# Attention and gated MLP on one core: weights converted in pieces of 1024 words, all orders new

## The chip, the cores and the metric

The kernel runs on one NeuronCore of a Trainium2 chip. Five engines work side by side: TensorE (PE, matrix multiplications), VectorE (DVE), ScalarE (ACT), GpSimd (POOL) and SyncE (SP, which here issues the DMAs). [...] The metric is device time in microseconds; a profiled execution also has a span, from its first instruction to its last.

## The reference

There are 8 batches of 8 heads, 576 tokens, head width 64. For each head:

```
scores = q @ k.T / 8, causal, + min(-(cum_i - cum_j), 0)    # cum: running sum of max(s, 0)
attn   = softmax(scores);  x = attn @ v
```

The heads of a batch are joined to x (576 x 512), and then

```
h    = max(x @ w_in, 0)                                     # 512 -> 1024 features
gate = sigmoid(conv over 3 tokens of h, weights conv_w per feature)
out  = (h * gate) @ w_out                                   # 1024 -> 512
```

q, k, v and s are float32. w_in, conv_w and w_out come as float64, and the kernel turns them into float32 on the chip.

## The kernel before, in words

**Stages.** 64 heads are worked as 32 pairs (`pair`, line 965): the score matmuls for the row maximum (line 1107), the maxima on DVE (lines 1124 and 1144), the scores again with the maximum subtracted (line 1231), the exponential on ACT (line 1248), the sums (line 1334) and the product with v (line 1282), then the division and the split of x into a high and a low part. After every four pairs a batch is complete; `moe_h` (line 1428) multiplies x with w_in (line 1447), applies the convolution (lines 1485 and 1501), the sigmoid (1516) and the product (1522) and splits the result into u (lines 1531 and 1536); `moe_o` multiplies u with w_out (line 1601). Matmuls are done in three products of high and low parts, so weights too are held as a high part in the matmul's rounded format and a low part, the rest: `wi` and `wo`.

**Converting the weights.** `weight_piece` (line 820) makes a chain of tasks for one piece. SP loads the float64 words into a staging buffer (line 845), each word as two 32-bit halves. ACT takes the absolute value of the upper halves (851), DVE or POOL raises it to a floor (855), DVE shifts it (861), puts the sign in (867) and the top bits of the lower half (873). ACT or DVE then writes the high part (909 for w_in, 930 for w_out), POOL or DVE the low part (912 and 933). DVE alone can do lines 861, 867 and 873. w_in is converted in 8 pieces, one for each tile of 128 features, 512 words wide in each partition. w_out is converted in 12: feature tiles 4 to 7 as pieces of 512 words, tiles 0 to 3 in two halves of 256 words. Pieces of 512 words use three buffers `w`, pieces of 256 words (and the small conv_w) three buffers `ht`. A buffer is free again when its piece's last step is done.

**Who needs them.** The matmuls of `moe_h` for two feature tiles need the pieces of both. The first write of u in batch 0 waits for all pieces (`first`, line 1528), because u lies in the memory that the staging buffers give back.

**The order.** Every instruction belongs to a task with a due time: a formula, plus a shift from the table `DUE`, found by a search. `Sched.play` imitates the engines: at each moment an engine takes the ready task that is due first and whose buffers are free, and where a task may run on several engines, the one that comes to it first. The order that results is written out for every engine before the kernel is built; the engines keep to it. If PE has nothing ready, an idle matmul (line 1667) is put in. SP's loads wait for the first bias rows (`dq0`), except a few early ones, among them the w_in pieces named in `FIRST`, here 5 and 6.

Of the kernel before, what the change touches and what calls it, by code (L numbers as in the profile page):

```python
# [29 lines left out]
FIRST = (5, 6)  # L30
# [65 lines left out]
    "pads":  # L96
        "0 141.6 1 -96.93 2 30.09",
    "ind":
# [400 lines left out]
def kernel(  # L499
# [404 lines left out]
    for f in range(NF):  # L904
# [6 lines left out]
        def fin_lo(e, w, fs=fs):  # L911
# [7 lines left out]
            prev=None,  # L919
        )  # L920
    for ch in range(2):
        for f in range(NF):
            wide = f >= WPN
            if wide and ch:
                continue
# [819 lines left out]
```

## Time and profile before

| | |
|---|---|
| timed runs (3), median, lowest, highest | 760.77, 757.41, 761.85 us |
| profiled execution: its time, its span | 757.21, 755.5 us |
| busy: PE, DVE, ACT, POOL | 729.3, 545.4, 390.0, 334.3 us |
| granted TensorE clock, mean | 0.998 |
| DMA, mean over the span | 100 GB/s |

PE is busy for nearly the whole span, but its busy time includes the idle matmuls, which compute nothing that is used. A stretch is therefore read in two steps: how long PE was busy in it, and how much of that was line 1667. For the other engines the busy share of a stretch tells whether they can be what is late in it; a share of the whole span mixes stages with different limits. In a timeline, a bracket behind a row gives the idle time ahead of it on that engine and what ended it.

### The profile page before, as it was taken

The numbers are of one execution on the slowest core, as the hardware profiler recorded it, in microseconds if no ns is written. First come the engines' busy times: TensorE is split into PE (matmuls) and PEld (weight loads), VectorE is DVE, ScalarE is ACT, GpSimd is POOL, SyncE is SP. The second block draws the span as 40 slices with busy tenths as digits, with TensorE's granted clock in tenths as the row PEclk, the third lists the DMA queues.
The fourth block names the chain that finished last, engine by engine and source line by source line (L and its number), as shares of the span: only waits on it lengthen the run. The fifth ranks groups of instructions, "written<-read, shape, count | busy, mean of one in ns | idle before, by whom it ended". The sixth has DMA issues, their size and how long they took to land. (4 is left out here: it accounts for less than half of the span.)

```text
span 755.5 us, 24083 instructions
## 1 busy us (share of the span) xinstructions
PE 729.3 (97%) x9930; PEld 612.0 (81%) x9930; DVE 545.4 (72%) x1441; ACT 390.0 (52%) x668; POOL 334.3 (44%) x457
## 2 busy tenths in 40 slices
PE   8999999999999999989999999899999999999998
PEld 6777787878878988878788798687988788788896
DVE  7899898776768777886874787556977589454632
ACT  6566475527636634746466265272736347343421
POOL 5544443134645551446748349285443345520000
PEclk9999999999999999999999999999999999999999
DMA  7666532125233332225314414323234222120010
GB/s 218 213 179 196 188 109 72 56 75 168 63 99 125 103 110 83 97 86 168 92 54 128 131 52 112 108 87 128 56 98 122 88 62 70 37 61 30 2 43 30
DMA packets 50089, 75.49 MB, mean 100 GB/s; under 512 B 13690, under 2 KB 26298, under 8 KB 49978
## 3 DMA queue, kind: packets, MB, share of 16 engines
q1 hardware_dynamic: 49960, 73.92, 32.5%
q8 instruction: 78, 1.28, 0.7%
q14 instruction: 33, 0.27, 0.1%
q10 hardware_dynamic: 18, 0.02, 0.0%
HBM read 63.53 MB, written 10.03 MB: 97 GB/s over the span
## 5 line engine op out<-in xcount | busy, mean ns | idle before, releaser
L1447 PE MATMUL ps<-x,wi 64*128 64x258 f32 (+1 forms) x3072 | 227.8, 298 | 2.7 <-DVE ct L1522 1.9
L1447 PEld LDWEIGHTS ps<-x,wi 64*128 64x128 f32 x3072 | 213.9, 187 | 8.9 <-DVE ct L1522 3.4
L1601 PE MATMUL ps<-wo,u 64*128 64x512 f32 x1536 | 194.2, 392 | 1.5 <-ACT u L1531 0.8
L1601 PEld LDWEIGHTS ps<-wo,u 64*128 64x128 f32 x1536 | 140.5, 185 | 28.3 <-ACT u L1531 1.4
L1144 DVE CUSTOM_DVE_ANT_0 ps<-ps,rw 128x64 f32<-128x64 f32 (+4 forms) x250 | 109.2, 438 | 52.4 <-POOL rw L1065 20.6
L1248 ACT ACTIVATE pt<-ps,less 128x1024 f32<-128x1024 f32 (+1 forms) x128 | 116.8, 928 | 52.0 <-PE ps L1231 48.5
L1501 DVE SCALAR_TENSOR_TENSOR ct<-ps,cw_sb,ct 128x319 f32<-128x319 f32 (+3 forms) x256 | 116.0, 506 | 2.8 <-ACT ct L1483 2.7
L1231 PE MATMUL ps<-s 64*128 64x288 f32 (+4 forms) x1152 | 107.6, 299 | 4.8 <-DVE r L1124 1.6
L1065 POOL TENSOR_SCALAR_AFFINE_SELECT rw<-rw 128x256 f32<-128x256 f32 (+1 forms) x125 | 48.5, 397 | 138.9 <-DMA rw<-cum_d 51.6
L1231 PEld LDWEIGHTS ps<-s 64*128 64x128 f32 (+1 forms) x1152 | 81.4, 177 | 13.6 <-ACT pt L1248 3.2
L1282 PE MATMUL ps<-pt,v 128*32 128x448 f32 (+4 forms) x1536 | 92.4, 388 | 0.0
L1516 ACT ACTIVATE ct<-ct 128x640 f32<-128x640 f32 (+1 forms) x64 | 43.9, 685 | 75.0 <-DVE ct L1501 74.8
L1282 PEld LDWEIGHTS ps<-pt,v 128*32 128x32 f32 x1536 | 48.6, 110 | 41.8 <-issue 31.0
L1468 ACT ACTIVATE ps<-ps 128x642 f32<-128x642 f32 (+1 forms) x64 | 40.7, 637 | 70.6 <-PE ps L1447 66.9
L1259 POOL TENSOR_SCALAR_AFFINE_SELECT pt<-pt 128x256 f32<-128x256 f32 (+1 forms) x115 | 43.4, 399 | 66.9 <-ACT pt L1248 50.9
L1485 DVE TENSOR_SCALAR ct<-ps,cw_sb 128x256 f32<-128x256 f32 (+1 forms) x53 | 26.8, 513 | 57.4 <-ACT ct L1483 53.6
L1522 DVE TENSOR_TENSOR ct<-ct,ps 128x640 f32<-128x640 f32 (+1 forms) x64 | 48.0, 749 | 17.5 <-ACT ct L1516 17.1
L1297 POOL TENSOR_TENSOR ad<-ad,pt 128x128 f32<-128x128 f32 (+2 forms) x51 | 49.9, 978 | 24.1 <-DVE ad L1297 12.7
L1536 POOL TENSOR_TENSOR u<-ct,u 128x512 fp32r<-128x512 f32 x35 | 45.2, 1291 | 29.0 <-ACT u L1531 15.9
L1107 PE MATMUL ps<-s 64*128 64x288 f32 (+4 forms) x384 | 51.1, 319 | 6.4 <-DVE r L1144 3.0
L1231 PE MATMUL ps<-eq,ek 64*128 64x288 f32 (+1 forms) x360 | 49.5, 297 | 0.0
L1107 PEld LDWEIGHTS ps<-s 64*128 64x128 f32 x384 | 33.4, 186 | 16.7 <-DVE r L1144 5.5
(120 smaller groups left out, 969.5 us busy)
## 6 DMA issues: line engine op xcount, KB each, us to landing
raw<-qk SPq DMA_DIRECT2D x32, 576.0 KB
rw<-cum_d SPq DMA_DIRECT2D x25, 576.0 KB
v<-vp SPq DMA_DIRECT2D x32, 320.0 KB
rb<-ri_d SPq DMA_DIRECT2D x64, 144.0 KB
out<-ob SPq DMA_DIRECT2D x32, 256.0 KB
w<-w_in SPq DMA_DIRECT2D x8, 512.0 KB
ht<-w_out SPq DMA_DIRECT2D x8, 256.0 KB
w<-w_out SPq DMA_DIRECT2D x4, 512.0 KB
```

The source lines that it names most:

```text
L1065: nc.gpsimd.affine_select(out=RW_t[:, :, o : o + k], in_=RW_t[:, :, d : d + k], pattern=[[0, 2], [-1, k]], compare_op=ALU.is_ge, fill=NEG, ...
L1107: nc.tensor.matmul(dst[j], l, m, start=(k == 0), stop=(k == 1 or late))
L1144: nc.vector.tensor_tensor_reduce(out=bank(pb, j, o, o + c1 - c0), in0=bank(pb, j, o, o + c1 - c0), in1=add_, scale=1.0, scalar=acc if c0 e ...
L1231: nc.tensor.matmul(d, l, m, start=(k < 2), stop=(k >= len(steps) - 2 or (t == L and k < 2)), skip_group_check=t == L,)
L1248: nc.scalar.activation(PT_t[pts[0].slot][:, :, o : o + w], both(pb, 0, w), AF.Sigmoid, bias=less, scale=0.125,)
L1282: nc.tensor.matmul(bank(pvs, n, o0, o0 + c1 - c0)[gs], vt[0:jt, t, gs], PT_t[pts[0].slot][0:jt, g // 2, O_T[t] + c0 : O_T[t] + c1], start= ...
L1297: tt_on(e)(acc, PT_t[pts[0].slot][:, :, P:S] if t == 1 else acc, PT_t[pts[0].slot][:, :, O_T[t] : O_T[t] + W_T[t]], op=ALU.add,)
L1447: mm = nc.tensor.matmul(bank(hb, i, 0, XW[hf]), wi[rows[j], k_ // 2, c, f * P : f * P + P], x[rows[j]], start=not turned and k == 0, stop= ...
L1501: nc.vector.scalar_tensor_tensor(cc[:, lo:hi], h_[:, sh + lo : sh + hi], cw_sb[:, 3 * f + k : 3 * f + k + 1], cc[:, lo:hi], op0=ALU.mult, ...
L1522: nc.vector.tensor_tensor(cc, cc, both(hb, 2 * hf, 2 * hf + hw), op=ALU.mult)
L1536: tt_on(e)(uu[:, 1, i, :], C_t[ct.slot][:, i, k0:hw], uu[:, 0, i, :].bitcast(F32), op=ALU.subtract)
L1601: mm = nc.tensor.matmul(bank(pb2 if m else pb, m, 0, cw_), l, r, start=turned + fp + n == 0, stop=turned == 1 and fp == FP - 1 and n == le ...
```

## The change

The weights are converted in pieces of two feature tiles, 1024 words wide in each partition: w_in in 4 pieces, w_out in 4. There are two staging buffers `w`, each of 2048 + 1024 words, in place of three of 1024 + 512; of the buffers `ht` one small one is left, for conv_w. The matmuls of a pair of feature tiles depend on one piece. `FIRST` names the one w_in piece of tiles 4 and 5 in place of the pieces 5 and 6. The table `DUE` has new values throughout, so the order of tasks differs on every engine, and with it which engine does the steps that several can do. The arithmetic of each step is the same.

```diff
-FIRST = (5, 6)
+FIRST = (4,)
...
 DUE = {
     "x":
-        "s -18.91 clear -24.65 ident -84.98 tab -76.05 hot -56.43 unit -41.86 mrow -163.13 "
+        "s 12.03 clear 79.57 ident -169.51 tab -180.19 hot 120.36 unit -4.51 mrow -66.81 "
...
-    H_t = [ep.tile([P, 6 * P], F32, name=f"ht{i}") for i in range(NHT)]
+    H_t = [ep.tile([P, P], F32, name=f"ht{i}") for i in range(1)]
...
-        [wp.tile([P, n], F32, name=f"w{i}_{n}{k}") for k, n in enumerate((8 * P, 4 * P))]
-        for i in range(3)
+        [wp.tile([P, n], F32, name=f"w{i}_{n}{k}") for k, n in enumerate((16 * P, 8 * P))]
+        for i in range(2)
...
-    for f in range(NF):
-        fs = slice(f * P, (f + 1) * P)
+    for f in range(0, NF, 2):
+        fs = slice(f * P, (f + 2) * P)
         src = w_in.rearrange("(c p) f -> p c f", p=P)[:, :, fs]
...
-        t_wi[f] = weight_piece(
-            f"wi{f}", src, NC, 2 * WPC, fin_hi, fin_lo, WI0 + f * WI1,
+        t_wi[f] = t_wi[f + 1] = weight_piece(
+            f"wi{f}", src, NC, 4 * WPC, fin_hi, fin_lo, WI0 + f * WI1,
             prev=None,
         )
-    for ch in range(2):
-        for f in range(NF):
-            wide = f >= WPN
-            if wide and ch:
-                continue
-            cs = slice(0, DM) if wide else slice(ch * WPC, (ch + 1) * WPC)
-            src = w_out[f * P : (f + 1) * P, cs].rearrange("p (a b) -> p a b", a=1)
...
+    for f in range(0, NF, 2):
+        src = w_out[f * P : (f + 2) * P].rearrange("(a p) b -> p a b", p=P)
...
+        t_wo[f] = t_wo[f + 1] = weight_piece(
+            f"wo{f}", src, 2, 2 * DM, fin_hi, fin_lo, WO0 + f * WO1, prev=None,
+        )
+        staged.append(t_wo[f])
...
-                       [x_done[b * HP + c] for c in range(NC)] + [t_wi[2 * fp], t_wi[2 * fp + 1]],
+                       [x_done[b * HP + c] for c in range(NC)] + [t_wi[2 * fp]],
...
-                    deps += [t_wo[2 * fp + i, ch] for i in range(2) for ch in range(2)]
+                    deps += [t_wo[2 * fp]]
```

## Rows read from the trace of the kernel before

**Rows 1.** The page, busy time by engine, share of the span, instructions.
```profile
PE 729.3 (97%) x9930; PEld 612.0 (81%) x9930; DVE 545.4 (72%) x1441; ACT 390.0 (52%) x668; POOL 334.3 (44%) x457
```
**Rows 2.** Stretches: from:to, length, busy us by engine (instructions), clock, DMA share, GB/s.
```profile
20.00:100.00 80.00, 75.96 (x1277) 59.41 (x1277) 72.58 (x154) 48.18 (x79) 38.94 (x31) 1.00 0.61 186
100.00:120.00 20.00, 19.70 (x308) 15.95 (x306) 18.36 (x51) 12.28 (x23) 9.65 (x12) 1.00 0.29 83
120.00:740.00 620.00, 604.21 (x8110) 514.62 (x8107) 437.65 (x1201) 314.58 (x544) 275.97 (x390) 1.00 0.29 87
```
**Rows 3.** The same for line 1667 alone, the idle matmuls: PE, weight loads.
```profile
20.00:100.00 80.00, 9.59 (x69) 5.75 (x67) 1.00 0.61 186
...
120.00:740.00 620.00, 6.32 (x50) 4.50 (x51) 1.00 0.29 87
```
**Rows 4.** Tile w: count, ns min/median/max of one, first and last start, shape.
```profile
L867 DVE SCALAR_TENSOR_TENSOR w<-w,w x12: 671/683/705, 10.4 to 91.8; 128x512 uint32<-128x512 uint32 x12
...
L855 DVE TENSOR_SCALAR w<-w x4: 415/418/426, 9.5 to 59.6; 128x512 f32<-128x512 f32 x4
...
L930 DVE CAST wo<-w x3: 416/819/841, 66.8 to 85.7; 128x512 fp32r<-128x512 f32 x3
```
**Rows 5.** Tile ht, the same.
```profile
L867 DVE SCALAR_TENSOR_TENSOR ht<-ht x9: 174/417/625, 20.1 to 106.7; 128x256 uint32<-128x256 uint32 x8, 128x24 uint32<-128x24 uint32 x1
```
**Rows 6.** Timeline of DVE, 27 to 57 us: start, length, line, operation, tiles.
```profile
27.33 0.67 DVE L867 SCALAR_TENSOR_TENSOR w<-w,w 128x512 uint32<-128x512 uint32 x1
27.93 0.74 DVE L987 CAST s<-raw 128x1152 fp32r<-128x1152 f32 x1
...
47.00 0.43 DVE L861 TENSOR_SCALAR w<-w 128x512 uint32<-128x512 uint32 x1 [0.36 <-POOL w L855]
47.34 0.28 DVE L861 TENSOR_SCALAR ht<-ht 128x256 uint32<-128x256 uint32 x1
47.54 0.68 DVE L867 SCALAR_TENSOR_TENSOR w<-w,w 128x512 uint32<-128x512 uint32 x1
...
56.09 0.42 DVE L867 SCALAR_TENSOR_TENSOR ht<-ht 128x256 uint32<-128x256 uint32 x1
56.43 0.28 DVE L1124 TENSOR_REDUCE r<-ps 128x2 f32<-128x128 f32 x1
```
**Rows 7.** Timelines of SP and DVE: two pieces' loads and their last steps.
```profile
54.04 1.04 SPq L845 DMA_DIRECT2D w<-w_out  x2
...
67.47 0.68 DVE L933 TENSOR_TENSOR wo<-w,wo 128x512 fp32r<-128x512 f32 x1
...
78.83 0.40 SPq L845 DMA_DIRECT2D w<-w_in  x1
...
104.36 0.68 DVE L912 TENSOR_TENSOR wi<-w,wi 128x512 fp32r<-128x512 f32 x1
```
**Rows 8.** Timeline of all engines, 116 to 126 us.
```profile
116.59 1.43 POOL L933 TENSOR_TENSOR wo<-ht,wo 128x256 fp32r<-128x256 f32 x2 [2.15 <-DVE rb L1391]
...
124.61 1.59 PE L1447 MATMUL ps<-x,wi 64*128 64x258 f32 x22 [0.83 <-DVE ct L1522]
```
**Rows 9.** Timeline of ACT, 1 to 10 us.
```profile
8.21 0.68 ACT L851 ACTIVATE w<-w 128x512 f32<-128x512 f32 x1
9.43 0.68 ACT L851 ACTIVATE w<-w 128x512 f32<-128x512 f32 x1 [0.54 <-DMA w<-w_in]
```
**Rows 10.** Timeline of PE, 464 to 488 us.
```profile
464.17 1.61 PE L1447 MATMUL ps<-x,wi 64*128 64x258 f32 x24
...
480.44 0.40 PE L1107 MATMUL ps<-s 64*128 64x288 f32 x2 [1.65 <-ACT vc L1388]
481.85 0.80 PE L1107 MATMUL ps<-s 64*128 64x448 f32 x4 [1.02 <-DVE r L1144]
482.46 2.79 PE L1447 MATMUL ps<-x,wi 64*128 64x258 f32 x24
```
**Rows 11.** Stretches of 4 us, columns as in rows 2.
```profile
480.00:484.00 4.00, 2.54 (x20) 2.29 (x22) 3.20 (x14) 0.76 (x3) 1.06 (x3) 0.69 0.04 8
```

More of the change, by code (lines that the diff above doesn't have):

```diff
@@ L92 @@
     "x":
[3 rows of a table removed]
[3 rows of a table added]
     "pads":
-        "0 141.6 1 -96.93 2 30.09",
+        "0 -154.47 1 -50.84 2 138.58",
     "ind":
[1 row of a table removed]
[1 row of a table added]
     "cw":
[1 row of a table removed]
[1 row of a table added]
     "wi":
[3 rows of a table removed]
[2 rows of a table added]
     "wo":
[6 rows of a table removed]
[2 rows of a table added]
     "qk":
[9 rows of a table removed]
[9 rows of a table added]
     "hi":
[4 rows of a table removed]
[4 rows of a table added]
     "lo":
[4 rows of a table removed]
[4 rows of a table added]
     "dr":
[4 rows of a table removed]
[4 rows of a table added]
     "dp":
[1 row of a table removed]
[1 row of a table added]
     "dq":
[1 row of a table removed]
[1 row of a table added]
     "eq":
[4 rows of a table removed]
[4 rows of a table added]
     "sh":
[4 rows of a table removed]
[4 rows of a table added]
     "tn":
[4 rows of a table removed]
[4 rows of a table added]
     "sc":
[4 rows of a table removed]
[4 rows of a table added]
     "pv":
[4 rows of a table removed]
[4 rows of a table added]
     "nm":
[4 rows of a table removed]
[4 rows of a table added]
     "fo":
[4 rows of a table removed]
[4 rows of a table added]
     "vn":
[4 rows of a table removed]
[4 rows of a table added]
     "rw":
[3 rows of a table removed]
[3 rows of a table added]
     "rk":
[16 rows of a table removed]
[14 rows of a table added]
 }
@@ L621 @@
         "rb": Pool(1), "ad": Pool(1), "r8": Pool(2), "rt": Pool(1), "ri": Pool(1), "rw": Pool(1), "u": Pool(NRING), "us": Pool(1),
-        "ht": Pool(NHT), "ct": Pool(NHT), "ob": Pool(NOB), "vc": Pool(1), "qsh": Pool(2), "qsc": Pool(2), "qh": Pool(2), "qo": Pool(1),
-        "w": Pool(3),
+        "ht": Pool(1), "ct": Pool(NHT), "ob": Pool(NOB), "vc": Pool(1), "qsh": Pool(2), "qsc": Pool(2), "qh": Pool(2), "qo": Pool(1),
+        "w": Pool(2),
     }
@@ L833, in parts @@
             wd = H_t[wd_.slot][:, 0 : 2 * n].bitcast(U32)
-            wc = H_t[wd_.slot][:, 4 * P : 4 * P + n].bitcast(U32)
+            wc = H_t[wd_.slot][:, 2 * n : 3 * n].bitcast(U32)
             return wd.rearrange("p (c t) -> p c t", t=2), wc
@@ L915, in fin_lo, with fin_hi @@
             )
-        t_wi[f] = weight_piece(
-            f"wi{f}", src, NC, 2 * WPC, fin_hi, fin_lo, WI0 + f * WI1,
+        t_wi[f] = t_wi[f + 1] = weight_piece(
+            f"wi{f}", src, NC, 4 * WPC, fin_hi, fin_lo, WI0 + f * WI1,
             prev=None,
         )
-    for ch in range(2):
-        for f in range(NF):
-            wide = f >= WPN
-            if wide and ch:
-                continue
-            cs = slice(0, DM) if wide else slice(ch * WPC, (ch + 1) * WPC)
-            src = w_out[f * P : (f + 1) * P, cs].rearrange("p (a b) -> p a b", a=1)
-            def fin_hi(e, w, f=f, cs=cs):
-                copy_on(e)(wo[:, 0, f, cs], w)
-            def fin_lo(e, w, f=f, cs=cs):
-                tt_on(e)(wo[:, 1, f, cs], w, wo[:, 0, f, cs].bitcast(F32), op=ALU.subtract)
-            t_wo[f, ch] = weight_piece(
-                f"wo{f}.{ch}", src, 1, DM if wide else WPC, fin_hi, fin_lo,
-                WO0 + (8 * ch + f) * WO1, prev=None,
-            )
-            if wide:
-                t_wo[f, 1] = t_wo[f, 0]
-            staged.append(t_wo[f, ch])
+    for f in range(0, NF, 2):
+        src = w_out[f * P : (f + 2) * P].rearrange("(a p) b -> p a b", p=P)
+        def fin_hi(e, w, f=f):
+            copy_on(e)(wo[:, 0, f : f + 2, :], w.rearrange("p (a b) -> p a b", a=2))
+        def fin_lo(e, w, f=f):
+            tt_on(e)(
+                wo[:, 1, f : f + 2, :], w.rearrange("p (a b) -> p a b", a=2),
+                wo[:, 0, f : f + 2, :].bitcast(F32), op=ALU.subtract,
+            )
+        t_wo[f] = t_wo[f + 1] = weight_piece(
+            f"wo{f}", src, 2, 2 * DM, fin_hi, fin_lo, WO0 + f * WO1, prev=None,
+        )
+        staged.append(t_wo[f])
     x_bufs, x_done = {}, {}
@@ L1526, in moe_h @@
         t_m = add(f"mu{b}.{hf}.{fp}", [("DVE", c_tt(2 * hw) + 0.03)], [t_g], tg, mul, uses=[ct, hb, q])
-        first = [t_m] + (list(t_wi.values()) + staged + last_sh if b == 0 else [])
+        first = [t_m] + (list(dict.fromkeys(t_wi.values())) + staged + last_sh if b == 0 else [])
         def u_hi(e):
```

159 rows, old and new, of the table DUE are left out of this document.

## The prediction, made before the changed kernel was seen

> **What bounds the kernel now.** First the page: TensorE (PE) is busy for 729.3 us, 97% of the span [rows 1]. That is not all useful work. The second view is the table by stretches; the reader is to compare PE's busy time there [rows 2] with the busy time of line 1667 alone [rows 3], the idle matmuls that the kernel issues when PE has nothing to do. Between 20 and 100 us PE is busy for 75.96 of 80, of which 9.59 are idle matmuls: 4.04 + 9.59 = 13.6 us, 17%, do nothing for the result. Between 120 and 740 us it is 15.8 idle and 6.32 idle matmuls, 22.1 of 620, or 3.6%. So the late part is bound by PE itself. In the early part something else is late, and the same rows name it: VectorE (DVE) is busy for 72.58 of 80 us and for 18.36 of the next 20, 91%, while ScalarE (ACT) has 60% and GpSimd (POOL) 49% [rows 2]. There DVE does the attention's row maxima and, beside them, the conversion of the weights. That is where this change acts.
>
> **The change part by part.** (1) Fewer, longer instructions. Now there are 12 pieces of 512 words and 8 of 256 (8 of w_in, 4 + 8 of w_out); after it 8 pieces of 1024. Each has three steps that only DVE can do (lines 861, 867, 873), and four (abs, floor, the two finishing steps) that are shared out. What a merge saves is the fixed part of an instruction. By durations it is 151 ns: 683 for 512 words and 417 for 256, so 266 for 256 words more and 151 left [rows 4, 5]. But DVE starts the next instruction before the one before is at its end, so I go by start to start, back to back: line 867 with 512 words 27.33 to 27.93, 0.60 us; with 256 words 56.09 to 56.43, 0.34; line 861 with 512 words 47.00 to 47.34, 0.34, and with 256 words 47.34 to 47.54, 0.20 [rows 6]. Fixed part: 2 x 0.34 - 0.60 = 0.08, and 0.06. A piece of 512 words costs DVE 0.34 + 0.60 + 0.60 = 1.54, one of 256 costs 0.20 + 0.34 + 0.34 = 0.88 (line 873 has the kind of operation and the size of 867), and by the same slopes one of 1024 costs 0.62 + 1.12 + 1.12 = 2.86. Sum now 12 x 1.54 + 8 x 0.88 = 25.5 us, then 8 x 2.86 = 22.9: 2.6 us saved. Of the shared steps DVE has some (the floor of 4 of the 12 larger pieces [rows 4]); at a quarter of all 80, an estimate, since the order decides, 20 now and 8 after, 12 go at 0.07 each: 0.8. DVE saves 3.4 us, all of it before 118 us. From above the bound is 151 ns for each of these 48, 7.2 us; from below nothing, should the order give DVE more of the shared steps.
>
> [...]
>
> What is it worth? In 20 to 120 us DVE is occupied 91% of the time, so of 3.4 us about 3.1 come off the stage (at most the 13.6 us that PE wastes there could come off). I take **-3.1**, with -7.2 and 0 as ends.
>
> (2) ACT and POOL lose their share of fixed parts too. I cost that at nothing: at 60% and 49% [rows 2] their slack hides it. If that cover is gone, a piece's chain is late by the extra length of one instruction on each.
>
> (3) Two buffers in place of three plus three small ones. A piece holds its buffer from the issue of its load to its last step: from 54.04 to 68.15 is 14.1 us, from 78.83 to 105.0 is 26.2 [rows 7]; the middle is 20. Twice the words add 2.8 us of load (0.52 MB more at 186 GB/s [rows 2]), 1.3 on DVE, and at most some 4 on ACT and POOL: about 28. Eight pieces through two buffers are four rounds; from 2 to 118 us there is room for 29 each. It just fits, so I take **0**, with 26.2 + 8 = 34 each, a delay of 4 x (34 - 29) = 20 us in the staging, as the worst end. Behind the last piece waits the first step that writes u (u lies in the staging's memory), behind u the gate's buffers, behind them the next x*w_in matmuls.
>
> (4) The end of the staging. The last weight step ends at 118.02, and PE's first wait behind that is 0.83 us at 124.61, for the gate [rows 8]. With DVE 3 us ahead it should go: **-0.8**, ends -0.8 and 0 (if it stays, what is late is the gate's own chain on DVE).
>
> (5) The start. Ahead of the bias rows there is now one load of 1 MB in place of two of half. The two halves are taken up by ACT at 8.21 and at 9.43 [rows 9], the second having waited for its load; one load can be begun only when all has landed, so its chain starts 1.2 us later, nearer to the first row maxima that DVE has to do. I take **+0.5**, ends 0 and +1.2. The loads move the same bytes, with runs twice as long; SP issues 12 fewer (0.4 us each [rows 7]), beside its own idle time: 0.
>
> (6) All priorities are new, so every engine's order changes. The trace cannot price an order that it does not show. Its ends come from the 22.1 us of waste between 120 and 740: half of it won is -11; two or three more stalls like the one described below [rows 10] are +8 to +12. Value **0**, the nearest row being the order that is there.
>
> Sum: -3.1 + 0 - 0.8 + 0.5 + 0 = **-3.4 us**. The profiled execution took 757.21 us (span 755.5 and 1.7 around it), so it would take 753.8; that run lies below all three timed ones, whose median is 760.77, 3.56 above. On that scale the forecast is 760.8 - 3.4 = 757.4, and I say **757.2**.
>
> **The rivals.** *A: nothing comes through.* The saved DVE time turns into idle matmuls, since the early stage ends with a given set of attention tiles and the late part is PE's. For it: 97% of PE, and 0.83 us is the one longer wait behind the staging. Against: 13.6 us of waste just where DVE is full. Time 760 to 763. Chance 0.15.
>
> *B: the order gives more.* The fixed part counts in full (7.2), or the new order finds part of the 22 us. For it: waits of that stretch come from chains that an order can shift [rows 10]. Against: the waste is spread over 620 us, and much of it must go at once. Time 760.8 - 3.4 - 5 and below: 745 to 753. Chance 0.23.
>
> *C, slower: one more long stall in the late part.* The place is a head pair's turn in 120 to 740: the row-maximum matmuls (line 1107) wait for a PSUM bank held by the copy of the attention output, and nothing else is ready. [...] Together 1.65 + 1.02 + 1.18 = 3.9 us. It decides from the second such stall: one more only eats the 3.4 gained, two give 760.8 - 3.4 + 7.8 = 765, four 773. For it: one is there now, and an order that serves DVE's long conversions can as easily make them. Against: just one in 620 us. Chance 0.17.
>
> [...] Time up to 760.8 + 10 = 771. Chance 0.05. [...]
>
> **How the numbers follow.** The forecast (752.5 to 760) has 0.40, half of it below the bound of 0.5% (757.0), half within. Faster by over 0.5%: 0.20 + 0.23 = 0.43. Within 0.5% (757.0 to 764.6, about what a measurement of this kernel can tell from no change): 0.20 + 0.11 of A = 0.31. Slower: 0.04 of A + 0.17 + 0.05 = 0.26. The range of 8 in 10 takes in the larger part of B, C and D: 747 to 769; the forecast's own is 752.5 to 760.
>
> **What would show it.** In the profile after: line 867 eight times with 1024 words at about 1.2 us; idle matmuls and idle time between 20 and 100 us down from 13.6 to about 10.5; the last weight step before 116; no wait of a new kind for a weight buffer; the waste of 120 to 740 at about 22. The forecast is wrong if DVE's time before 120 falls and the 13.6 stays (A), or if the late waste moves by more than 4 us either way (B, C); then the order and not the pieces has decided.

## The result and the profile after

The changed kernel took 748.15 us (median of 4 runs, 746.52 to 749.44) against 759.64 (4 runs, 757.41 to 761.85): a ratio of 0.985 [0.981, 0.989], 11.5 us faster. Its profiled execution took 747.92 us, the span 746.0. Forecast: 757.2, range 747 to 769. The time lies inside that range, near its lower end, in rival B (745 to 753, "the order gives more", chance 0.23) and outside the forecast's own range of 752.5 to 760.

The page after, which answers to [rows 1]: TensorE (PE) does the same work in 6.3 us less busy time; VectorE (DVE) is as busy as before in 34 fewer instructions.

```profile
PE 723.0 (97%) x9916; PEld 609.1 (82%) x9916; DVE 545.7 (73%) x1407; ACT 380.6 (51%) x632; POOL 339.6 (46%) x445
```

The stretches after, columns as in [rows 2], and behind them the same view for the idle matmuls alone (line 1653 now), as [rows 3].

```profile
20.00:100.00 80.00, 78.13 (x1314) 62.00 (x1314) 63.77 (x119) 50.70 (x67) 50.11 (x28) 1.00 0.61 188
100.00:120.00 20.00, 20.00 (x324) 16.34 (x320) 19.21 (x41) 11.32 (x21) 9.94 (x9) 1.00 0.39 110
120.00:740.00 620.00, 602.81 (x8103) 514.23 (x8101) 447.11 (x1218) 305.30 (x525) 271.04 (x386) 1.00 0.28 86
740.00:746.00 6.00, 5.01 (x46) 3.89 (x42) 0.69 (x1) 0.58 (x1) 0.00 (x0) 1.00 0.23 87
```
```profile
20.00:100.00 80.00, 11.03 (x82) 7.19 (x82) 1.00 0.61 188
100.00:120.00 20.00, 0.00 (x0) 0.00 (x0) 1.00 0.39 110
120.00:740.00 620.00, 3.86 (x29) 2.51 (x29) 1.00 0.28 86
740.00:746.00 6.00, 3.67 (x32) 3.05 (x32) 1.00 0.23 87
```

Waste (idle plus idle matmuls) between 20 and 100 us is 1.87 + 11.03 = 12.90, 0.7 less than before, although DVE is busy for 8.8 us less there. The reader is to see POOL's column too: it rose from 38.94 to 50.11. A part of what left DVE went there; the subtraction that splits the raw scores is one such operation, 7 times on DVE in the first 120 us of before, 3 times after (tile s of DVE: before, then after).

```profile
L993 DVE TENSOR_TENSOR s<-raw,s x7: 1339/1348/1358, 8.1 to 103.1; 128x1152 fp32r<-128x1152 f32 x7
```
```profile
L979 DVE TENSOR_TENSOR s<-raw,s x3: 1348/1350/1359, 8.1 to 74.7; 128x1152 fp32r<-128x1152 f32 x3
```

Between 120 and 740 the waste is 17.19 + 3.86 = 21.05, 1.1 less. That seems to leave the 9.5 us by which the span shrank without a place. Two things fill it. Behind 740 us PE still had useful work in the kernel before; in the new one it ends at 741.41 instead of 749.83. The ends in PE's timeline, before and after (L1667 and L1653 idle matmuls):

```profile
736.95 1.93 PE L1601 MATMUL ps<-wo,u 64*128 64x512 f32 x12 [0.25 <-ACT u L1531]
738.81 2.68 PE L1667 MATMUL ps<-mask 128*128 128x256 bf16 x23
742.06 7.78 PE L1601 MATMUL ps<-wo,u 64*128 64x512 f32 x60 [0.56 <-ACT u L1531]
```
```profile
728.18 0.50 PE L1653 MATMUL ps<-mask 128*128 128x256 bf16 x3
...
729.84 11.57 PE L1587 MATMUL ps<-wo,u 64*128 64x512 f32 x95 [0.73 <-DVE ob L1619]
```

From 740 us to the end of the span the waste fell from 2.7 + 5.16 = 7.9 us to 0.99 + 3.67 = 4.7. Summed over all stretches it fell by 5.3; the other 4.2 us left what the table calls useful busy time. Most of that is one line, the row-maximum matmuls, 51.1 us busy before and 47.7 after for the same 384 instructions. Of the widest of them (448 columns) 36 of 64 took over 0.43 us before and 18 after, most others about 0.36; what makes them longer these rows do not show. So useful busy time is not a fixed measure of work, and the table by stretches cannot place the gain.

To see where the lead arises I gave each useful matmul the mean time that its kind takes when nothing is waited for, and compared when the two kernels reach the same sum. The new one is 1.9 to 3.5 us ahead at 110 to 140 us, nearly level at 290, 3 to 4 ahead at 390 to 415, 7 at 493 (behind the stall of [rows 10], which is gone), 4 at 567, 8 at 645 and at 748. So no single place makes the gain: it comes and goes with the order, and about 7 us of it arise behind 264 us, where no weight is converted any more. Each trace is one execution: e4, e9, e10 and e11 below, which do up to 222 us just what the kernel before does, stand 1.4 to 2.5 us behind its trace between 112 and 222 us. A lead of 2 us there tells little by itself; the late part is steadier (see e7).

### The profile page after: what moved, and what is told of

It reads as the page before. It is cut to its first block, busy times and chain, and to the rows that moved or that the text cites. A ratio compares the mean times of both kernels' runs of the same rounds, so it can differ in the third digit from the quotient of the medians.

```text
span 746.0 us, 23942 instructions
## 1 busy us (share of the span) xinstructions
PE 723.0 (97%) x9916; PEld 609.1 (82%) x9916; DVE 545.7 (73%) x1407; ACT 380.6 (51%) x632; POOL 339.6 (46%) x445
## 5 line engine op out<-in xcount | busy, mean ns | idle before, releaser
L1130 DVE CUSTOM_DVE_ANT_0 ps<-ps,rw 128x448 f32<-128x448 f32 (+4 forms) x250 | 109.7, 439 | 51.9 <-POOL rw L1051 17.4
L1217 PE MATMUL ps<-s 64*128 64x288 f32 (+4 forms) x1152 | 107.9, 298 | 3.8 <-ACT pt L1234 1.7
L1217 PEld LDWEIGHTS ps<-s 64*128 64x128 f32 (+1 forms) x1152 | 81.5, 177 | 11.2 <-ACT pt L1234 3.5
L1283 POOL TENSOR_TENSOR ad<-ad,pt 128x640 f32<-128x640 f32 (+2 forms) x62 | 64.0, 1033 | 11.9 <-DVE ad L1283 4.5
L1471 DVE TENSOR_SCALAR ct<-ps,cw_sb 128x256 f32<-128x256 f32 (+1 forms) x61 | 30.4, 510 | 49.5 <-ACT ct L1469 43.4
L1522 POOL TENSOR_TENSOR u<-ct,u 128x512 fp32r<-128x512 f32 x33 | 42.5, 1288 | 45.2 <-DVE u L1517 24.5
L979 POOL TENSOR_TENSOR s<-raw,s 128x1152 fp32r<-128x1152 f32 x17 | 46.2, 2716 | 25.2 <-ACT s L973 17.9
L1093 PE MATMUL ps<-s 64*128 64x288 f32 (+4 forms) x384 | 47.7, 309 | 5.2 <-DVE r L1130 4.9
```

Of the source, the lines that this page charges most:

```text
L1093: nc.tensor.matmul(dst[j], l, m, start=(k == 0), stop=(k == 1 or late))
L1130: nc.vector.tensor_tensor_reduce(out=bank(pb, j, o, o + c1 - c0), in0=bank(pb, j, o, o + c1 - c0), in1=add_, scale=1.0, scalar=acc if c0 e ...
L1217: nc.tensor.matmul(d, l, m, start=(k < 2), stop=(k >= len(steps) - 2 or (t == L and k < 2)), skip_group_check=t == L,)
L1283: tt_on(e)(acc, PT_t[pts[0].slot][:, :, P:S] if t == 1 else acc, PT_t[pts[0].slot][:, :, O_T[t] : O_T[t] + W_T[t]], op=ALU.add,)
```

## The experiments

All ran in 5 rounds beside the kernel before; ratios are to it. Where an order is transplanted, the planner's run is replaced by a list of all tasks with their engine, so that two plans can be cut and joined:

```diff
-    order = sch.play(
-        (AWAKE, t_ident, 0.005 + AWAKE_N * 0.42e-3, AWAKE_T, stay_awake, pool_ps)
-    )
+    order = replay()          # tasks in the sequence and on the engines of ORDER
```

**The pieces alone: e1.** The changed kernel and its order, each conversion step issued as two halves.

```diff
-                nc.vector.tensor_scalar(
-                    wb, wb, 3, 0x3FFFFFF8, op0=ALU.logical_shift_left, op1=ALU.bitwise_and,
-                )
+                for r in halves(n):
+                    nc.vector.tensor_scalar(
+                        wb[:, r], wb[:, r], 3, 0x3FFFFFF8, op0=ALU.logical_shift_left, op1=ALU.bitwise_and,
+                    )
...
```

> The changed kernel with its order kept, but each of the seven conversion steps of a 1024-word piece made as two instructions of 512 words (the loads and the buffers stay as they are). It gives back the fixed parts and nothing else: 56 instructions more, some 35 of them on DVE. Theory P (the gain comes from the pieces, because DVE is what is late before 120 us): some 35 x 0.07 = 2.5 us to 35 x 0.15 = 5 us slower than the changed kernel's 748.2, so 750.5 to 753. Theory O (the gain comes from the new order of everything else): 748 to 749, no difference that can be told.

750.56 us (750.08 to 752.54), ratio 0.9887 [0.9868, 0.9905]. The medians differ from the changed kernel's by 2.4 us, the ratios by 0.0039 x 760 = 3.0. The intervals of the two ratios overlap a little, but all six runs of e1 lie above all four of the changed kernel. Its page:

```profile
PE 724.3 (97%) x9916; PEld 606.9 (81%) x9916; DVE 548.2 (73%) x1440; ACT 382.1 (51%) x646; POOL 341.9 (46%) x454
```

33 more instructions on DVE make it busy for 2.5 us more, 0.076 us each: the distance of starts (0.06 to 0.08 from [rows 6]) and not the 0.15 of the durations. DVE's weight steps went from 83 instructions to 38, so e1 puts back 33 of 45; the benefit of longer instructions is 2.4 to 3.0 us by e1 and an estimated 3.3 to 4.1 in full (by 45/33). So 2.5 us less work for DVE were worth about as much time. Some 7 to 8 of the 11.5 lie elsewhere.

**The order alone: e2.** The new order of the other tasks, with the old pieces and their conversion tasks at the times where the kernel before had them.

```diff
-ORDER: the old plan (pieces of 512 and 256 words)
+ORDER e2 (old pieces): the new plan, weight tasks at their old times
```

> The pieces, loads, buffers and conversion tasks of the kernel before, put at the times where the kernel before had them; all other tasks in the order of the changed kernel, on the engines where it has them. Theory P: 757 or more, since the old pieces are back. Theory O: the new order is what counts, so 748 to 752, with up to 3 us for tasks that get in each other's way because nobody fitted this mixture together.

769.88 us, ratio 1.0136 [1.0115, 1.0157]: slower. The loss is in the head:

```profile
20.00:100.00 80.00, 71.19 (x1136) 55.54 (x1134) 63.81 (x122) 41.88 (x69) 41.00 (x33) 0.91 0.56 167
100.00:120.00 20.00, 16.66 (x206) 12.86 (x204) 17.25 (x38) 12.44 (x18) 13.47 (x10) 1.00 0.33 101
```

By 112 to 140 us it is some 20 us behind the kernel before; behind 164 us it regains some 8. The first says only that my mixture fits neither order, and not what the pieces or the order are worth; the second I read as the late order's gain.

**Parts of the order: e3 to e7.** Plans joined at one point.

```diff
-ORDER: the plan of one kernel from start to end
+ORDER e3 (pieces of 1024): new until 222 us, then old
+ORDER e4 (old pieces):     old until 657 us, then new
+ORDER e5 (pieces of 1024): new until 424 us, then old
+ORDER e6 (pieces of 1024): new until 656.5 us, then old
+ORDER e7 (old pieces):     old until 222 us, then new
```

> The changed kernel (new pieces and new order) up to the tasks planned for 222 us, which is behind all conversions, then the order of the kernel before. Theory P: the whole gain is made by then: 748 to 750. Theory O: the two traces stand only 1.5 to 3 us apart between 110 and 240 us, so 756 to 758.5, and the rest of the gain is missing.

756.27 us, ratio 0.9954 [0.9931, 0.9976]: the new head, with the longer pieces in it, is worth 3.5 us (1.8 to 5.2 by the interval), no more than the pieces alone give. The joint does not hide more: in the trace its lead over the kernel before is 0.6 us at 222 us and 0.8 at the end.

> The kernel before up to the tasks planned for 657 us, where both orders have done exactly the same tasks, then the tail of the changed kernel's order. Theory P: 759 to 760, no gain. Theory O: the last 90 us hold 2 us (by the distance of the traces at the cut) to 4.4 us (by the idle time and idle matmuls behind 740 us) of the gain: 755 to 758.

758.80 us, ratio 0.9993 [0.9969, 1.0017]: no difference that can be told.

> As the experiment with the new head (new pieces, new order up to 222 us), but the new order goes on up to the tasks planned for 424 us; then the order of the kernel before. That one measured 756.3. If the order's gain is spread evenly over the work behind 222 us (some 8 us over 520), 424 us should be reached 3 us earlier: 752.5 to 754.5. If it lies in one or two stalls behind 424 us, as the one at 480 us in the kernel before, nothing is added: 756 to 757.

759.40 us, ratio 0.9996 [0.9973, 1.0019]. In the trace it follows the changed kernel until about 440 us, 5.8 us ahead of the kernel before; by 460 us it has lost 5 of these, by 645 us all. The seam eats what the first half had won.

> The changed kernel up to the tasks planned for 656.5 us, then the tail of the kernel before, with its waits of PE at 737 and 742 us. By the experiment that put the new tail behind the old kernel (0.7 us gained, within its interval) 748 to 750. By the distance of the two traces in the tail, 2 to 4.4 us: 750 to 752.5.

750.89 us, ratio 0.9881 [0.9862, 0.9899]: 0.0033 or 2.5 us behind the changed kernel, so the new tail may be worth about that behind the new middle; the intervals of the two ratios overlap, and e4 shows nothing of it behind the old middle.

> The kernel before, with its old pieces, up to the tasks planned for 222 us, then the order of the changed kernel to the end. If the parts add, it lacks just the 3.5 us that the new head was worth: 751 to 752.5, and the order behind 222 us is worth 7 to 8 us by itself. If the later order only pays behind its own head, 755 or more.

763.60 us, ratio 1.0061 [1.0038, 1.0084]. Here the seam is seen in the open. PE's timeline:

```profile
237.42 0.32 PE L1431 MATMUL ps<-ident,r 64*68 64x64 f32 x2 [5.37 <-DVE r L1409]
...
247.27 0.88 PE L1496 MATMUL ps<-s 64*128 64x448 f32 x6 [2.89 <-DVE ct L1787]
```

and the stretch behind the first wait, with a granted clock of 0.50, after PE had been busy for 0.05 of the 4 us before (columns as in [rows 2]):

```profile
232.00:236.00 4.00, 0.05 (x2) 0.00 (x0) 1.78 (x5) 0.00 (x0) 0.00 (x0) 0.87 0.10 25
236.00:240.00 4.00, 2.58 (x24) 2.58 (x26) 2.36 (x8) 2.22 (x5) 0.41 (x1) 0.50 0.37 111
```

The joint costs 12 to 15 us; from 264 us to the end the same kernel regains 7.0, as the changed kernel does over the same stretch (from 1.4 to 8.4 ahead). Counted in this way, all five kernels with the new order from there to the end gain on the kernel before: the changed one 7.0, e1 6.7, e2 7.4, e7 7.0, e12 (below) 7.4. Three that have the old order there, e3, e8 and e9 (but for one move in SyncE's queue), stay within 0.5. So the late order is worth about 7 us, whether the kernel comes to it ahead or 20 us behind.

**Is DVE late in the early stage? e8.** The kernel before, its order kept, three of DVE's conversion steps cut down to two words:

```diff
-                    wb, wb, 3, 0x3FFFFFF8, op0=ALU.logical_shift_left, op1=ALU.bitwise_and,
+                    wb[:, 0:2], wb[:, 0:2], 3, 0x3FFFFFF8, op0=ALU.logical_shift_left, op1=ALU.bitwise_and,
...
```

> The kernel before with its order kept; the three conversion steps that only DVE does (shift, sign, low bits) work on 2 words of each piece in place of all 512 or 256, which leaves the rest of the float32 words as the floor step made them. It takes some 22 us of DVE's work away before 118 us. Theory P (DVE is what is late in the early stage): PE's waits there go, 4.3 us of idle time in 20 to 120 us; the idle matmuls are part of the order and stay, so 754 to 757. If DVE is not what is late: 759 to 760.

755.32 us, ratio 0.9943 [0.9926, 0.9959], so 4.3 us less. Its row as in [rows 2], then the idle matmuls as in [rows 3]:

```profile
20.00:100.00 80.00, 78.23 (x1319) 62.08 (x1319) 58.84 (x163) 50.61 (x82) 36.02 (x32) 1.00 0.66 190
20.00:100.00 80.00, 9.58 (x69) 5.74 (x67) 1.00 0.66 190
```

DVE lost 13.7 us of work there, and PE is 3.1 us ahead at 112 us and nearly stays so. Freeing DVE helps. But this run cannot give the rate: the 69 idle matmuls are written into the order and stay (9.59 us before, 9.58 here), so only PE's idle time could go, 4.04 + 0.30 = 4.3 us between 20 and 120 us, of which 1.99 are left.

**The worst stall of before by itself: e9 to e12.** The changed kernel's trace has no wait like that of [rows 10]. What stood behind it? DVE's timeline of the kernel before shows that the copy that PE waited for was itself behind a transfer, the spread of the reciprocals (rb<-ri_d):

```profile
478.05 0.76 DVE L1391 TENSOR_TENSOR rb<-vc,rb 128x576 f32<-128x576 f32 x1 [4.37 <-DMA rb<-ri_d]
...
480.72 0.47 DVE L1144 CUSTOM_DVE_ANT_0 ps<-ps,rw 128x288 f32<-128x288 f32 x1 [0.55 <-DMA rw<-cum_d]
```

e9 moves three big transfers in SyncE's order behind it, e10 does so in eight turns, e11 gives PE other work ahead of the waiting matmuls, e12 is e10's move in the changed kernel.

```diff
-fo21 qk26 st3.1.0 st3.1.1 ri21 rb21 rw24      (e9, SyncE: ri21 stores, rb21 spreads,
+fo21 ri21 rb21 qk26 st3.1.0 st3.1.1 rw24       qk raw scores, st output, rw row windows)
-o4.0.0.10 sh24.1 sh24.2 h4.1.2 sh24.3 o4.0.0.11   (e11, PE: sh row maxima,
+o4.0.0.10 h4.1.2 o4.0.0.11 sh24.1 sh24.2 sh24.3    h x*w_in, o u*w_out)
```

> The kernel before with its order of work kept, but on SyncE's queue one 576 KB load of raw scores and two 256 KB output stores, which in the one bad late turn (476 to 484 us) stand ahead of the small store of the reciprocals and of the load that spreads them, are moved behind that load. Theory Q (in that turn VectorE waits 4.37 us for the spread reciprocals because their small store, sent at 466.77, queued behind the big transfers and the load could start only at 472.88; the PSUM bank that TensorE waits for comes free only after it; the new order wins mainly by not having this): the stall of 476 to 484 goes, 2 to 4 us less, 755.5 to 757.5 against 759.6. Theory R (the late part is bound by other things, a stall removed comes back later): 759 to 761.

759.31 us, ratio 0.9993 [0.997, 1.0016]: no difference that can be told. The wait changed its name (DVE, then PE, of e9):

```profile
477.01 0.76 DVE L1657 TENSOR_TENSOR rb<-vc,rb 128x576 f32<-128x576 f32 x1 [1.53 <-DMA rb<-ri_d]
...
482.46 0.47 DVE L1410 CUSTOM_DVE_ANT_0 ps<-ps,rw 128x288 f32<-128x288 f32 x1 [3.33 <-DMA rw<-cum_d]
```
```profile
483.60 0.80 PE L1373 MATMUL ps<-s 64*128 64x448 f32 x4 [2.86 <-DVE r L1410]
```

DVE waited 4.37 + 0.55 = 4.92 us for transfers before and 1.53 + 3.33 = 4.86 now. The reciprocals come earlier, the windows (rw, 576 KB) by as much later.

> The same move in every late turn of the kernel before where a load of raw scores or an output store stands between the two ends of the reciprocals' round trip (8 turns). Theory Q: as for one turn and some more, since four turns show this wait (11.3 us of VectorE in sum, of which TensorE felt about half): 753 to 757. Theory R: 759 to 761; slower than 761 if the loads moved back are themselves late.

762.14 us, ratio 1.0012 [0.9995, 1.003]. In another turn the moved load makes a new stall: DVE waits 4.57 us for rw at 438.01 and PE 2.79 at 439.14.

> The kernel before with the order of TensorE alone changed in the one bad late turn: 24 matmuls of x*w_in (1.6 us) and 6 of u*w_out (0.9 us), which stood behind the row-maximum matmuls that wait for the PSUM bank, go ahead of them. If what TensorE lacked there was only something ready to do: 2 to 3 us less, 756.5 to 758 against 759.6. If the late thing is the chain behind the bank (row maxima on VectorE), they only fill the hole and the chain ends as late as before: 759 to 760.5.

761.58 us, ratio 1.0026 [1.0003, 1.005]: if anything slower. The filler was not ready either:

```profile
482.65 1.71 PE L1713 MATMUL ps<-x,wi 64*128 64x258 f32 x24 [2.34 <-ACT rt L1443]
...
487.31 0.50 PE L1373 MATMUL ps<-s 64*128 64x320 f32 x4 [1.20 <-DVE r L1410]
489.38 0.66 PE L1497 MATMUL ps<-s 64*128 64x288 f32 x6 [1.57 <-DVE r L1410]
```

It waited 2.34 us for ACT, which stood behind the same late product on DVE, and the chain of row maxima then ended later still.

> The changed kernel with the same move on SyncE's queue in its nine late turns, the last one included (two output stores around the last store of reciprocals, VectorE waiting 2.44 us for the load at 675.6). Theory Q: the changed kernel has only 4.2 us of such waits left, most of it in the last turn: 746 to 748 against 748.15, at best a small gain. Theory R: 748 to 749; slower if a raw load is then late.

748.18 us, ratio 0.9848 [0.9824, 0.9872], the changed kernel's own. No version here beats it.

My theory for these four, that the new order wins by keeping one kind of transfer out of another's way, is not borne out: repaired locally, the stall comes back under another name (e9, e10), and the changed kernel gains nothing from the same move (e12).

## Why the prediction went as it did

The sign was right, the mechanism forecast was there, and its size nearly so; the step that failed is (6), the order, put at 0 with ends of -11 and +12. It was worth some 7 us. That 748.15 us still lies in the stated range of 747 to 769 is owed to rival B, for which the range was made wide, and not to the sum: it had -3.4 us, and -11.5 were measured.

(1) *Longer instructions, -3.1*: right. e1 measures 2.4 to 3.0 for 33 of the 45, and 45 at 0.076 are the 3.4 us of DVE that the sum had. The three steps cost what the slopes gave: with 1024 words they take 0.69, 1.22 and 1.22 us, and where the next instruction follows at once the starts lie 0.60 us (the shift) and 1.13 to 1.14 us (the other two) apart, where the sum had 0.62 and 1.12 (tile w after, answering to [rows 4]; in line 848 is what the order gave DVE and POOL of the floor):

```profile
L854 DVE TENSOR_SCALAR w<-w x8: 673/692/695, 10.6 to 104.0; 128x1024 uint32<-128x1024 uint32 x8
L860 DVE SCALAR_TENSOR_TENSOR w<-w,w x8: 1151/1220/1226, 12.6 to 106.0; 128x1024 uint32<-128x1024 uint32 x8
L866 DVE SCALAR_TENSOR_TENSOR w<-w,w x8: 1211/1219/1964, 17.3 to 114.5; 128x1024 uint32<-128x1024 uint32 x8
L848 POOL TENSOR_SCALAR w<-w x6: 2758/2766/3537, 22.1 to 96.0; 128x1024 f32<-128x1024 f32 x6
L848 DVE TENSOR_SCALAR w<-w x2: 695/702/708, 9.9 to 86.0; 128x1024 f32<-128x1024 f32 x2
```

By the durations of [rows 4, 5], a fixed part of 151 ns each, e1's 33 further instructions would have been 5.0 us of DVE; its trace has 2.5. For this saving by merging, the distance of starts was the right price. The argument that brought it over, "DVE is 91% occupied, so 91% come off the stage", fits e1, where 2.5 us of DVE cost 2.4 to 3.0 us of time; e8, with its idle matmuls fixed, cannot test it. But the sign that I named, waste down to 10.5 between 20 and 100 us, did not show: it is 12.90, in e1 2.91 + 10.33 = 13.2. That row varies too much from one execution to the next to carry 3 us: with the head of the kernel before it reads 12.6 in e11 and 15.9 in e10.

(2) *ACT and POOL, 0*: nothing speaks against it; e1 splits their steps too (ACT 14 instructions more and 1.5 us busier than in the changed kernel, POOL 9 and 2.3), so their part lies within its 2.4 to 3.0. No run has it by itself.

(3) *Two buffers, 0*: nothing speaks against it; no run has it by itself. Their eight loads are issued at 2.05, 13.67, 25.85, 35.91, 44.44, 67.93, 74.91 and 86.69 us, and the last step ends 0.5 us later than before, not 20.

(4) *The end of the staging, -0.8*: the wait of [rows 8] went, but not for the reason given. The last weight step starts at 117.28 and takes 1.23, to 118.51 where it was 118.02 and "before 116" was forecast; yet PE waits for nothing between 100 and 133 us. Here the stage's last step said little about who waits for it.

(5) *The start, +0.5*: too much. The one load is taken up at 8.70, between the 8.21 and 9.43 of [rows 9], and up to 20 us PE does as much useful work as before (3.93 us against 16.64 - 12.66 = 3.98).

(6) *The order, 0*: the failure. Taking the value of "the order that is there" amounted to saying that a new order is as likely to lose as to win. The row that could have warned was [rows 10]: a stall that PE could not fill, left over in the old order. Of the 11.5 us 3 to 4 are the pieces (e1, e3) and some 7 arise behind 264 us, in many small places. How much of these is the tail is not settled: e6 gives 2.5, e4 0.5 with an interval that holds 0. What in the new middle makes it so is open: repairing the one stall or the queue's order in the old kernel (e9 to e11) gave nothing. The sign named for this case, the late waste moving by more than 4 us, failed too: between 120 and 740 us it moved by 1.1, since both kernels are compared there over the same time and not over the same work.

The rivals: A is refuted by the time itself and by e1 and e3. C did not come: PE has no wait over 1.4 us behind 120. The 3.9 us that it counts for one stall are the waits of 1.65 and 1.02 us in [rows 10] and the 1.18 us that 24 matmuls took longer at 482.46 than at 464.17 us, with a granted clock of 0.69 on average in 480 to 484 us [rows 11]. D (up to 771 us) did not come either, and its 10 us are shown by no run: between 20 and 100 us POOL was busy for 11.2 us more (50.11 after 38.94), and PE's idle time there fell from 4.04 to 1.87; what some DVE steps lost beside a step of POOL, 0.21 to 0.74 us each, stands in the last section. B described the result, but for half a wrong reason: the fixed part does not count in full; it was the order.

## What to carry to other kernels

Price a merge of small instructions by the distance of their starts (here 0.06 to 0.08 us for one instruction less where the durations say 0.15, and e1 measured 0.076), and check it by splitting them again with the order kept. When a planner lays the order anew, give that a term with its own chance: it can outweigh the edit that set it off. Parts of an order cannot always be bought singly: of the five joints here two cost some 6 and 12 to 15 us (e5, e7), the others (e3, e4, e6) no more than about 1 in their traces. Before repairing the longest wait, follow it back to what is shared behind it; here that was a transfer queue, and moving transfers in it only renamed the wait (4.92 us of DVE's before, 4.86 in e9).

## What the hardware showed beside it

In these traces some operations with two sources on DVE took longer when they began while POOL was in an operation of its own, and others did not. DVE and POOL in the changed kernel:

```profile
30.96 1.96 DVE L866 SCALAR_TENSOR_TENSOR w<-w,w 128x1024 uint32<-128x1024 uint32 x1
...
59.33 1.21 DVE L866 SCALAR_TENSOR_TENSOR w<-w,w 128x1024 uint32<-128x1024 uint32 x1
```
```profile
29.20 2.65 POOL L979 TENSOR_TENSOR s<-raw,s 128x1152 fp32r<-128x1152 f32 x1 [2.68 <-PE ps L1093]
...
58.38 2.77 POOL L848 TENSOR_SCALAR w<-w 128x1024 f32<-128x1024 f32 x1
```

At 30.96 POOL's subtraction had 0.89 us to run, and the DVE step took 0.74 more than its 1.22; at 59.33 POOL's one-source step had 1.82 to run, and DVE's took its normal time, 1.21. Three more starts behind a POOL TENSOR_TENSOR in this trace (at 102.27, 114.50 and 123.53 us) were late by 0.13 to 0.14 us less than what POOL had left (0.62, 0.45 and 0.61 of 0.76, 0.58 and 0.75); the convolution's steps (line 1487) begun during POOL's sum at 108.10 to 109.48 us were not late and took 0.54 us each. One of POOL's affine selects, which have one source, shows the same: a sum begun on DVE at 112.25 us, with 0.35 of a select to run, took 0.21 longer. So the number of POOL's sources does not tell the cases apart: six of the seven two-source steps that DVE began during a floor step took their normal time (the seventh, at 96.67 us, took 0.25 more, with 2.11 to run); in the kernel before 10 of 14 did. What sets them apart is not shown.
